# K in place: the score matmuls read 32 consecutive keys at a time, one exp per pair, p turned by four matmuls

## The chip, the cores and the metric

The kernel runs on one core of a Trainium2 chip. The metric is the device time of one execution in microseconds; a kernel is run several times and the median is given. One further execution is profiled. Engines are named as in the profile: PE is TensorE (PEld its weight loads), DVE is VectorE, ACT is ScalarE, POOL is GpSimd, SP is SyncE, which issues the DMAs.

## The reference

Two decode layers, run twice over the same weights and caches. Four tokens (one per batch entry, B = 4), width 448, 16 query heads over 8 key/value heads of size 256, the last 2048 keys of an 8192-key cache, and an FFN of 1792:

```python
W = min(4096, max(256, Sk // 4))                     # 2048
q = (x @ wq).reshape(B, Sq, 16, 256).transpose(0, 2, 1, 3)
k = repeat(k_cache[:, :, Sk - W:, :], 2, axis=1)
v = repeat(v_cache[:, :, Sk - W:, :], 2, axis=1)
p = softmax(einsum("bhqd,bhkd->bhqk", q, k) * 256 ** -0.5)
o = einsum("bhqk,bhkd->bhqd", p, v)
attention = o.transpose(0, 2, 1, 3).reshape(B, Sq, 4096) @ wo
ffn = (silu(x @ w_gate) * (x @ w_up)) @ w_down

x = x + attention(layernorm(x)); x = x + ffn(layernorm(x))
x = x + attention(layernorm(x)); x = x + ffn(layernorm(x))
```

All inputs and the output are bfloat16.

## The kernel before

The unit of work is a *pair*: one token and one key/value head (two query heads) in one of the two layers, so 2 x 4 x 8 = 64 pairs. A token's K and V for one head are 1 MB each and come as two loads of 512 KB each, into `half` buffers (27 of them, 4 KB per partition, shared by K and V). For 5 of 8 heads, K and V loaded in layer 0 are held until the token's pair of layer 1 has used them; the other 3 are loaded again. So 44 pairs load and 20 reuse, and up to 20 of the 27 buffers are held.

A step of the loop is one head: at the ends one pair, in the middle two, the earlier token in layer 1 and the next token in layer 0. When a token has done all 8 heads, its residual, norm, FFN, next norm and query projection (`ffn`, `qproj`, L482 and L523 and L551) come between the pairs.

One pair (`pair`, from L608) goes as follows.

- SP issues two K loads (L616) and two V loads (L629), each waiting for the release of the buffer that it fills. SP's instructions run in order.
- K arrives with 16 consecutive keys per partition, 8 in each half. DVE transposes each half in place in 32 x 32 blocks of 4-byte words (L621), so that partitions run over the head dimension and columns hold the keys. In a half, a column index splits into `(l g c r v)`: `l` (2) and `g` (4) name the key in its partition, `c` the block of the head dimension, `r` (32) the partition that the key came in, `v` the element of the 4-byte word.
- POOL builds `qe` (L646), the query masked so that 8 columns hold the four partition quadrants for two heads. PE computes the scores (L642, `scores`): 32 matmuls, 8 (`ce`) x 2 halves (`hf`) x 2 (`x`). Each has 8 stationary columns and 128 moving columns; the four of one `ce` write to partitions 0, 32, 64 and 96 of one PSUM tile, and the 8 accumulate. This group of 32 is called a burst below.
- DVE takes the maximum over 128 columns (L653), PE spreads it over partitions (L656), DVE makes the bias (L660, L664), ACT takes the exp (L668), once for each half of K, 40 partitions each, into `praw`. In `praw` the columns are ordered `(g r h l)`, so that the two halves alternate in pairs of columns; what a half does not own stays zero.
- PE turns p with two matmuls (L677), `praw` stationary and a selection matrix `selt` moving; ACT copies the result to `pT` (L684). PE sums p (L687), DVE and POOL make the reciprocal (L692, L710).
- PE multiplies by V (L700, `pv`): 16 matmuls of 4 stationary and 256 moving columns, again four side by side in four partition quadrants. ACT and DVE take the sum out (L712, L714), PE flips it (L720), DVE scales it into `oT` (L725), and PE does the output projection of the step (L745).

No order is written out by hand. Each operation is recorded in a graph with an engine, a planned duration, a rank (`pos` and leads such as `SLEAD`) and what it reads and writes. `Graph.schedule` plays this graph with the planned durations, takes on each engine the ready operation of lowest rank, chooses the buffer that is planned to come free first for each load, and so fixes every engine's order and the semaphore waits. Planned durations therefore decide the order on PE and SP. Before, a score burst is planned at `32 * MM` with `MM = 0.034`, an exp at 0.33 and the turn at 0.08 us.

Of the kernel before, what the change touches and what calls it, by code (L numbers as in the profile page):

```python
# [5 lines left out]
ACT = mybir.ActivationFunctionType  # L6
ALU = mybir.AluOpType
AX = mybir.AxisListType
BF16 = mybir.dt.bfloat16
# [24 lines left out]
SLEAD = 2.5  # L34
# [4 lines left out]
NS = 2  # L39
# [8 lines left out]
PE, DVE, SCA, POOL, SP = "pe", "dve", "act", "pool", "sp"  # L48
# [230 lines left out]
def build(nc, A_x, A_k_cache, A_v_cache, A_wq, A_wo, B_x, B_w_gate, B_w_up, B_w_down, out):  # L279
    s0 = A_k_cache.shape[2] - WIN  # L280
    g = Graph()

    with ExitStack() as es:
        def sb(name, shape, dt):
            return es.enter_context(nc.sbuf_tensor(name, shape, dt))
# [5 lines left out]
        wd_sb = sb("wd_sb", [128, NFC, D], BF16)  # L291
        half = [sb(f"half{s}", [128, 8 * DH], BF16) for s in range(NPOOL)]
        identb = sb("identb", [128, 128], BF16)
        onesb = sb("onesb", [128, 1], BF16)
        rab = sb("rab", [128, 129], BF16)
        ra = [rab[:, 1:129], rab[:, 0:128]]
        esel = sb("esel", [128, 4, 4, 32], BF16)
        selt = sb("selt", [128, 2, 4, 2, 2], BF16)
        small = sb("small", [128, 11 + 6 * NS + 4 * NY], FP32)
        nmask = small[:, 9 + 2 * NS + 4 * NY:11 + 2 * NS + 4 * NY]  # L300
        nbias = small[:, 11 + 2 * NS + 4 * NY:11 + 6 * NS + 4 * NY]
# [2 lines left out]
        negm = [small[:, 6 + 2 * i:8 + 2 * i] for i in range(NS)]  # L304
        rs = [small[:, 6 + 2 * (NS + i):8 + 2 * (NS + i)] for i in range(NY)]
        ri = [small[:, 6 + 2 * (NS + NY + i):8 + 2 * (NS + NY + i)] for i in range(NY)]
        qmask = sb("qmask", [128, 4], BF16)
        qc = [sb(f"qc{t}", [128, HKV, 8, 2], BF16) for t in range(B)]
        qe = [sb(f"qe{i}", [128, 8, 4, 2], BF16) for i in range(NQ)]
        qS = sb("qS", [128, 8, 16], BF16)  # L310
# [7 lines left out]
        xb = sb("xb", [128, 4, B], BF16)  # L318
        th = sb("th", [128, 2 * NFC], FP32)
        hT = sb("hT", [128, 2 * NFC], BF16)  # L320
        pmax = [sb(f"pmax{s}", [128, 1], BF16) for s in range(NS)]
        praw = [sb(f"praw{s}", [128, 256], BF16) for s in range(NS)]
        pT = [sb(f"pT{s}", [128, 2, 2, 4, 2, 2], BF16) for s in range(NY)]
        oh = [sb(f"oh{s}", [128, DH], BF16) for s in range(NY)]
        osel = sb("osel", [128, 2], BF16)
        oT = [sb(f"oT{s}", [128, 2, 2, 2], BF16) for s in range(2)]

        def ps(name):
            return es.enter_context(nc.psum_tensor(name, [128, 512], FP32))

        Sb = [ps(f"S{i}") for i in range(NS)]
        Yb = [ps(f"Y{i}") for i in range(NY)]
# [4 lines left out]
        R0 = -100.0  # L337
        MM = MMV
# [24 lines left out]
        for a in range(4):  # L363
            g.op(DVE, 0.1, R0, lambda e, a=a: e.memset(qmask[32 * a:32 * a + 32, a:a + 1], DH ** -0.5), r=("qmask",),
                 w=(f"qmask{a}",))
        ivt = identb[:, :].rearrange("p (h x z n) -> p h x z n", h=2, x=2, n=2)
        for y in range(2):
            for x in range(2):
                g.op(DVE, 0.1, R0, lambda e, y=y, x=x: e.tensor_reduce(
                    selt[:, x, :, y, :], ivt[:, :, x, 0:4, :].rearrange("p h a n -> p a n h"), AX.X, ALU.max),  # L370
                    r=("identb",), w=(f"selt{y}{x}",))
        idq = identb[:, :].rearrange("p (q z n) -> p q z n", q=4, n=2)
        g.op(DVE, 0.2, R0, lambda e: e.tensor_reduce(
            nmask[:, :], idq[:, :, 0:4, :].rearrange("p q a n -> p n q a"), AX.XY, ALU.add), r=("identb",), w=("nmask",))
        for s_ in range(NS):
            g.op(DVE, 0.2, R0, lambda e, s_=s_: e.memset(Sb[s_][:, :], 0.0), w=(f"s{s_}",), bank=(f"S{s_}",))
            g.op(DVE, 0.2, R0, lambda e, s_=s_: e.memset(praw[s_][:, :], 0.0), w=(f"praw{s_}_0", f"praw{s_}_1"))
        for a in range(4):
            g.op(DVE, 0.2, R0, lambda e, a=a: e.tensor_copy(
                esel[:, :, a, :], identb[:, :].rearrange("p (c s) -> p c s", c=4)), r=("identb",), w=(f"esel{a}",))  # L380
# [3 lines left out]
            w=("osel",))  # L384
        g.op(DVE, 0.2, R0, lambda e: e.tensor_reduce(lomask[:, :], iv[:, :, 1, :], AX.XY, ALU.add), r=("identb",),
             w=("lomask",))
# [199 lines left out]
        def x_in(e):  # L586
            last = None
            for cc in range(4):
# [6 lines left out]
             r=("z",), w=tuple(f"x{t}" for t in range(B)), bank=("Z",))  # L595
# [10 lines left out]
        pos = -1  # L606

        def pair(pos, si, side, nside, t, layer, kvh):  # L608
            p_, s_, q_ = pos % NY, pos % NS, pos % NQ
            if layer == 1 and (t, kvh) in k_held:  # L610
                kc, kk = k_held.pop((t, kvh))
            else:
                kc, kk = [[], []], [f"k{pos}_{hf}" for hf in range(2)]
# [21 lines left out]
            def scores(e):  # L635
                last = None
                for ce in range(8):
                    for hf in range(2):
                        kt = half[kc[hf][0]][:, :].rearrange("p (l g c r v) -> p c v g r l", l=2, g=4, c=4, v=2)
                        for x in range(2):  # L640
                            qd = 64 * hf + 32 * x
                            last = e.matmul(Sb[s_][qd:qd + 8, 0:128], lhsT=qe[q_][:, ce, :, :].rearrange("p a n -> p (a n)"),  # L642
                                            rhs=kt[:, ce // 2, ce % 2, 2 * x:2 * x + 2, :, :], start=(ce == 0),
                                            stop=(ce == 7), skip_group_check=True)
                return last
            g.op(POOL, 0.25, pos - SLEAD - 1, lambda e: e.tensor_tensor(  # L646
                qe[q_][:, :, :, :], qc[t][:, kvh, :, :].unsqueeze(2).broadcast_to([128, 8, 4, 2]),
                qmask[:, :].unsqueeze(1).unsqueeze(3).broadcast_to([128, 8, 4, 2]), op=ALU.mult),
                r=(f"qc{t}_{kvh}",) + tuple(f"qmask{a}" for a in range(4)), w=(f"qe{q_}",))
            o = g.op(PE, 32 * MM, pos - SLEAD, scores, r=tuple(kk) + (f"qe{q_}",), w=(f"s{s_}",), bank=(f"S{s_}",))  # L650
            if not keep_k:
                o.rel = tuple(kc)
            g.op(DVE, 0.21, pos, lambda e: e.tensor_reduce(  # L653
                pmax[s_][0:104, :], Sb[s_][0:104, 0:128], AX.X, ALU.max),
                r=(f"s{s_}",), w=(f"pmax{s_}",), bank=(f"S{s_}",))
            g.op(PE, 0.1, pos, lambda e: e.matmul(  # L656
                Sb[s_][0:104, 128:160].rearrange("p (q x) -> p q x", q=4), lhsT=pmax[s_][0:104, 0:1].broadcast_to([104, 104]),
                rhs=identb[0:104, :].rearrange("p (q x) -> p q x", q=4)[:, :, 0:8], start=True, stop=True,
                skip_group_check=True), r=(f"pmax{s_}", "identb"), w=(f"m{s_}",), bank=(f"S{s_}",))
            g.op(DVE, 0.16, pos, lambda e: e.tensor_reduce(  # L660
                negm[s_][0:104, :], Sb[s_][0:104, 128:160].rearrange("p (k n) -> p n k", n=2), AX.X, ALU.max, negate=True),
                r=(f"m{s_}",), w=(f"negm{s_}",), bank=(f"S{s_}",))
            nb = nbias[:, 4 * s_:4 * s_ + 4]
            g.op(DVE, 0.2, pos, lambda e: e.scalar_tensor_tensor(  # L664
                out=nb[0:104, 2:4], in0=negm[s_][0:104, :], scalar=1.0, in1=nmask[0:104, :], op0=ALU.mult, op1=ALU.mult,
                accum_out=nb[0:104, 0:1]), r=(f"negm{s_}", "nmask"), w=(f"nb{s_}",))
            for hf in range(2):
                g.op(SCA, 0.33, pos, lambda e, hf=hf: e.activation(  # L668
                    praw[s_][64 * hf:64 * hf + 40, :].rearrange("p (g r h l) -> p h g r l", g=2, h=2, l=2)[:, hf, :, :, :],
                    Sb[s_][64 * hf:64 * hf + 40, 0:128].rearrange("p (g r l) -> p g r l", g=2, l=2), ACT.Exp,  # L670
                    bias=nb[64 * hf:64 * hf + 40, 0:1]),
                    r=(f"s{s_}", f"nb{s_}"), w=(f"praw{s_}_{hf}",), bank=(f"S{s_}",))

            def turn(e):
                last = None
                for c in range(2):
                    last = e.matmul(Yb[p_][:, 64 + 32 * c:96 + 32 * c], lhsT=praw[s_][0:104, 128 * c:128 * c + 128],  # L677
                                    rhs=selt[0:104, :, :, :, :].rearrange("p x a y n -> p (x a y n)"), start=(c == 0),
                                    stop=False, skip_group_check=True)
                return last  # L680
            g.op(PE, 0.08, pos, turn,
                 r=(f"praw{s_}_0", f"praw{s_}_1") + tuple(f"selt{y}{x}" for y in range(2) for x in range(2)), w=(f"yp{p_}",),
                 bank=(f"Y{p_}",))
            g.op(SCA, 0.2, pos, lambda e: e.activation(  # L684
                pT[p_][:, :, :, :, :, :].rearrange("p c x a y n -> p (c x a y n)"), Yb[p_][:, 64:128], ACT.Copy),
                r=(f"yp{p_}",), w=(f"pT{p_}",), bank=(f"Y{p_}",))
            g.op(PE, 0.05, pos, lambda e: e.matmul(  # L687
                Yb[p_][:, 32:64].rearrange("p (k n) -> p k n", n=2), lhsT=onesb[:, 0:1].broadcast_to([128, 128]),
                rhs=pT[p_][:, :, :, :, :, :].rearrange("p c x a y n -> p y (c x a) n")[:, 0, :, :], start=False,
                stop=False, skip_group_check=True),  # L690
                 r=(f"pT{p_}", "onesb"), w=(f"ysum{p_}",), bank=(f"Y{p_}",))
            g.op(DVE, 0.18, pos, lambda e: e.tensor_reduce(  # L692
                rs[p_][:, :], Yb[p_][:, 32:64].rearrange("p (k n) -> p n k", n=2), AX.X, ALU.add),
                r=(f"ysum{p_}",), w=(f"rs{p_}",), bank=(f"Y{p_}",))

            def pv(e, hv):
                last = None
                for a in range(2):
                    for gg in range(4):
                        last = e.matmul(Yb[p_][32 * gg:32 * gg + 4, 256:512],  # L700
                                        lhsT=pT[p_][:, gg % 2, gg // 2, 2 * hv + a, :, :].rearrange("p y n -> p (y n)"),
                                        rhs=half[vs[hv][0]][:, 1024 * a + 256 * gg:1024 * a + 256 * gg + 256], start=False, stop=False, skip_group_check=True)
                return last
            for hv in range(2):
                kw = dict(acc=(f"y{p_}",)) if hv else dict(w=(f"y{p_}",))
                o = g.op(PE, 0.385, pos, lambda e, hv=hv: pv(e, hv), r=(f"pT{p_}", f"v{t}_{kvh}_{hv}"),
                         bank=(f"Y{p_}",), **kw)
                if not keep_v:
# [4 lines left out]
                 w=(f"oh{p_}",), bank=(f"Y{p_}",))  # L713
# [4 lines left out]
            def flip(e):  # L718
# [9 lines left out]
                r=(f"yo{p_}", f"ri{p_}"), w=(f"oT{si % 2}_{side}",), bank=(f"Y{p_}",))  # L728
# [24 lines left out]
        for si, pairs in enumerate(steps()):  # L753
# [8 lines left out]
            for t, layer in full:  # L762
                pos_ = pos
                pos = pos_ - CROSS
# [12 lines left out]
                pos = pos_  # L777
# [34 lines left out]
def bass_interleave_layers__sliding_block_cached__swiglu_ffn__decode_kernel(  # L812
    nc, A_x, A_k_cache, A_v_cache, A_wq, A_wo, B_x, B_w_gate, B_w_up, B_w_down, out
):
    build(nc, A_x, A_k_cache, A_v_cache, A_wq, A_wo, B_x, B_w_gate, B_w_up, B_w_down, out)
# [28 lines left out]
```

## Time and profile before

| | |
|---|---|
| median of 8 runs | 327.36 us (324.97 to 328.58) |
| profiled execution, its own time | 328.58 us |
| its span, first to last instruction | 326.7 us |
| mean granted TensorE clock | 0.741 of full |
| read from HBM | 104.44 MB, 320 GB/s over the span |
| busy: PE, PEld, DVE, ACT, POOL | 238.4, 169.2, 198.9, 90.9, 85.2 us |
| scores, L642 on PE | 2048 matmuls, 306 ns each |
| K transposes, L621 on DVE | 88, 1239 ns each |
| exp, L668 on ACT | 128, 362 ns each |
| turn, L677 on PE | 128 matmuls, 183 ns each, 101 ns for the weight load |

The span can be cut into 40 slices of 8.17 us; a digit is the busy share of a slice in tenths. "PEclk" is the clock that the throttle granted TensorE in that slice. A matmul's own duration includes its way through the array, and matmuls overlap, so what a row of matmuls costs is read from the time between starts. In a group's line, "x32" is the number of instructions and the number before it the time from the first start to the last end. In the chain of waits, "issue" is time in which an engine waited for nothing that the profile shows, and SPq is SP's queue of DMA issues.

### The profile page before, as it was taken

To read this page: it belongs to the slowest core of one execution; us is meant where nothing else is said; L and a number is where in the kernel's file an instruction comes from. 1 tells how busy PE (TensorE), PEld (TensorE's weight loads), DVE (VectorE), ACT (ScalarE), POOL (GpSimd) and SP (SyncE) were. 2 spreads that over 40 slices of the span, in tenths; PEclk is the share of its full clock that TensorE was granted. 3 is DMA by queue.
4 is the path that set the end of the run, shared out by engine and by line. 5 is a ranking of instruction groups with operands and counts; after the bars stand their busy time and mean duration, and the time that the engine had idled before them with its cause. 6 is when DMAs were issued, how large, how long until landed. Compare 5 with 4: busy or idle time off the path is not lost.

```text
span 326.7 us, 13161 instructions
## 1 busy us (share of the span) xinstructions
PE 238.4 (73%) x5792; PEld 169.2 (52%) x5792; DVE 198.9 (61%) x744; ACT 90.9 (28%) x289; POOL 85.2 (26%) x199
## 2 busy tenths in 40 slices
PE   2656555456578787797588887789878878689965
PEld 1534333244365555485455554566745556576545
DVE  6387556643145889773348798756567983834422
ACT  0313122111013344223143434122333443124510
POOL 2313211112020333223034332304143324134311
PEclk9998556777557999855579999555577997558955
DMA  7999999999989999997689998999599999735000
GB/s 281 391 404 392 393 397 394 393 398 393 395 309 315 378 374 369 402 358 264 243 294 403 400 401 304 398 391 387 195 392 368 350 376 396 256 106 221 2 2 2
DMA packets 42329, 105.28 MB, mean 322 GB/s; under 512 B 3097, under 2 KB 7201, under 8 KB 41889
## 3 DMA queue, kind: packets, MB, share of 16 engines
q1 hardware_dynamic: 42272, 104.45, 85.3%
q8 instruction: 45, 0.74, 0.9%
q14 instruction: 12, 0.09, 0.1%
HBM read 104.44 MB, written 0.00 MB: 320 GB/s over the span
## 4 chain that ended last, share of the span: by engine, by line
PE 34%; DMA 30%; DVE 13%; SPq 12%; issue 6%; ACT 3%
DMA half<-in_A_k_cache_dram 18%; DMA half<-in_A_v_cache_dram 13%; PE S L642 12%; DVE half L621 7%; PE Y L700 7%; SPq L616 6%; PE Z L482 4%; PE A L745 4%; SPq L629 3%; SPq L398 3%; DVE oh L714 2%; ACT praw L668 2%; PE Z L523 2%; PE Y L720 1%; PE Z L431 1%
## 5 line engine op out<-in xcount | busy, mean ns | idle before, releaser
L621 DVE STREAM_TRANSPOSE half<-half 128x1024 uint32<-128x1024 uint32 x88 | 109.1, 1239 | 24.0 <-DMA half<-in_A_k_cache_dram 23.5
L642 PE MATMUL S<-half,qe 128*8 128x128 bf16 x2048 | 84.9, 306 | 13.1 <-ACT praw L668 5.2
L700 PE MATMUL Y<-half,pT 128*4 128x256 bf16 x1024 | 53.3, 323 | 21.4 <-DMA half<-in_A_v_cache_dram 11.8
L642 PEld LDWEIGHTS S<-half,qe 128*8 128x8 bf16 x2048 | 51.8, 89 | 31.3 <-ACT praw L668 8.5
L710 POOL TENSOR_TENSOR small<-small 128x2 f32<-128x2 f32 x64 | 44.3, 696 | 75.9 <-DVE small L692 69.3
L668 ACT ACTIVATE praw<-S,small 40x128 bf16<-40x128 f32 x128 | 46.4, 362 | 46.7 <-DVE small L664 45.2
L712 ACT ACTIVATE oh<-Y 128x256 bf16<-128x256 f32 x64 | 24.4, 381 | 86.2 <-PE Y L700 85.8
L646 POOL TENSOR_TENSOR qe<-qc,qmask 128x64 bf16<-128x64 bf16 x64 | 18.6, 292 | 103.7 <-PE S L642 87.6
L653 DVE TENSOR_REDUCE pmax<-S 104x1 bf16<-104x128 f32 x64 | 18.4, 287 | 39.5 <-PE S L642 39.3
L714 DVE SCALAR_TENSOR_TENSOR oh<-oh,small,Y 128x256 bf16<-128x256 bf16 x64 | 30.0, 472 | 15.0 <-ACT oh L712 14.7
L700 PEld LDWEIGHTS Y<-half,pT 128*4 128x4 bf16 x1024 | 21.1, 86 | 29.3 <-DMA half<-in_A_v_cache_dram 13.4
L745 PE MATMUL A<-oT,wo_sb 128*128 128x1 bf16 (+1 forms) x688 | 24.3, 165 | 5.0 <-DVE oT L725 4.0
L745 PEld LDWEIGHTS A<-oT,wo_sb 128*128 128x128 bf16 x688 | 21.0, 99 | 11.2 <-DVE oT L725 6.1
L684 ACT ACTIVATE pT<-Y 128x64 bf16<-128x64 f32 x64 | 13.9, 222 | 45.5 <-PE Y L677 36.7
L720 PE MATMUL Y<-osel,oh 128*128 128x2 bf16 x128 | 12.2, 170 | 12.3 <-DVE oh L714 12.3
L687 PE MATMUL Y<-pT,onesb 128*128 128x32 bf16 x64 | 12.1, 191 | 9.6 <-ACT pT L684 9.5
L720 PEld LDWEIGHTS Y<-osel,oh 128*128 128x128 bf16 x128 | 7.6, 103 | 20.8 <-DVE oh L714 16.2
L449 POOL TENSOR_SCALAR st<-st 128x1 f32<-128x1 f32 x16 | 4.2, 265 | 50.5 <-DVE st L437 39.0
L482 PE MATMUL Z<-xn,wq_sb 128*128 128x1 bf16 (+1 forms) x480 | 15.5, 166 | 1.0 <-DMA wq_sb<-in_A_wq_dram 0.7
L656 PE MATMUL S<-identb,pmax 104*104 104x32 bf16 x64 | 13.4, 229 | 2.6 <-DVE pmax L653 1.1
L687 PEld LDWEIGHTS Y<-pT,onesb 128*128 128x128 bf16 x64 | 6.8, 108 | 15.9 <-ACT pT L684 12.4
L482 PEld LDWEIGHTS Z<-xn,wq_sb 128*128 128x128 bf16 x480 | 14.2, 104 | 1.5 <-DMA wq_sb<-in_A_wq_dram 0.8
(81 smaller groups left out, 232.6 us busy)
## 6 DMA issues: line engine op xcount, KB each, us to landing
half<-in_A_k_cache_dram SPq DMA_DIRECT2D x88, 512.0 KB, 7.3
half<-in_A_v_cache_dram SPq DMA_DIRECT2D x88, 512.0 KB, 7.2
wo_sb<-in_A_wo_dram SPq DMA_DIRECT2D x8, 448.0 KB, 12.4
wq_sb<-in_A_wq_dram SPq DMA_DIRECT2D x3, 1024.0 KB, 7.0
wd_sb<-in_B_w_down_dram SPq DMA_DIRECT2D x1, 1568.0 KB, 16.2
wg_sb<-in_B_w_gate_dram SPq DMA_DIRECT2D x1, 1344.0 KB, 14.2
wu_sb<-in_B_w_up_dram SPq DMA_DIRECT2D x1, 1344.0 KB, 14.7
wq_sb<-in_A_wq_dram SPq DMA_DIRECT2D x1, 512.0 KB, 10.4
```

The source lines that it names most:

```text
L482: last = e.matmul(o, lhsT=lhsT, rhs=rhs, start=(cc == 0 and hh == 0 and ee == 0), stop=(cc == 3), skip_group_check=True)
L616: g.dma(pos - KLEAD, 1 << 19, lambda e, cell=cell, hf=hf: e.dma_start(half[cell[0]][:, :], ksrc[:, 2048 * hf:2048 * hf + 2048]), None, w=( ...
L621: return e.transpose(a, a)
L642: last = e.matmul(Sb[s_][qd:qd + 8, 0:128], lhsT=qe[q_][:, ce, :, :].rearrange("p a n -> p (a n)"), rhs=kt[:, ce // 2, ce % 2, 2 * x:2 * x ...
L668: g.op(SCA, 0.33, pos, lambda e, hf=hf: e.activation(praw[s_][64 * hf:64 * hf + 40, :].rearrange("p (g r h l) -> p h g r l", g=2, h=2, l=2 ...
L687: g.op(PE, 0.05, pos, lambda e: e.matmul(Yb[p_][:, 32:64].rearrange("p (k n) -> p k n", n=2), lhsT=onesb[:, 0:1].broadcast_to([128, 128]), ...
L700: last = e.matmul(Yb[p_][32 * gg:32 * gg + 4, 256:512], lhsT=pT[p_][:, gg % 2, gg // 2, 2 * hv + a, :, :].rearrange("p y n -> p (y n)"), r ...
L710: g.op(POOL, 0.25, pos, lambda e: e.tensor_tensor(ri[p_][:, :], rs[p_][:, :], expo[:, 1:3], op=ALU.pow), r=(f"rs{p_}", "expo"), w=(f"ri{p_ ...
L712: g.op(SCA, 0.28, pos, lambda e: e.activation(oh[p_][:, :], Yb[p_][:, 256:512], ACT.Copy), r=(f"y{p_}",), w=(f"oh{p_}",), bank=(f"Y{p_}",))
L714: g.op(DVE, 0.4, pos, lambda e: e.scalar_tensor_tensor(out=oh[p_][:, :], in0=oh[p_][:, :], scalar=lomask[:, 0:1], in1=Yb[p_][:, 256:512], ...
L720: last = e.matmul(Yb[p_][:, 2 * dh:2 * dh + 2], lhsT=oh[p_][:, :].rearrange("p (m e) -> p e m", e=2)[:, dh, :], rhs=osel[:, :], start=Fals ...
L745: last = e.matmul(Av[:, cc, sl], lhsT=wo_sb[:, 4 * kvh + k, c0:c0 + 128], rhs=oT[si % 2][:, k % 2, k // 2, 0:n], start=False, stop=False, ...
```

## The change

The score matmuls read their moving operand in the order `(g l r)` instead of `(g r l)`: innermost, 32 keys that lie two elements apart, where before two keys 1024 elements apart alternated. The scores therefore stand in PSUM in another order, and the exp puts them back: it reads PSUM as `(g l r)` permuted to `g r l`, 32 words apart innermost. One exp now does both halves of K on partitions 0 to 103. Since both halves then lie in the same columns of `praw` (two columns wider, the first two zero), the turn has a selection matrix for each half and reads `praw` once from column 2 on and once from column 0 on, which moves the second half by two columns: four matmuls instead of two. The planned durations become 0.8, 0.38 and 0.12 us. Some one-column tiles share one tile, `tiny`.

```diff
-        onesb = sb("onesb", [128, 1], BF16)
+        tiny = sb("tiny", [128, 8 + NS], BF16)
+        onesb, qmask, osel = tiny[:, 0:1], tiny[:, 2:6], tiny[:, 6:8]
+        pmax = [tiny[:, 8 + s:9 + s] for s in range(NS)]
...
-        selt = sb("selt", [128, 2, 4, 2, 2], BF16)
+        selt = [sb(f"selt{h}", [128, 2, 4, 2, 2], BF16) for h in range(2)]
...
-        praw = [sb(f"praw{s}", [128, 256], BF16) for s in range(NS)]
+        praw = [sb(f"praw{s}", [128, 258], BF16) for s in range(NS)]
...
-        for y in range(2):
-            for x in range(2):
-                g.op(DVE, 0.1, R0, lambda e, y=y, x=x: e.tensor_reduce(
-                    selt[:, x, :, y, :], ivt[:, :, x, 0:4, :].rearrange("p h a n -> p a n h"), AX.X, ALU.max),
-                    r=("identb",), w=(f"selt{y}{x}",))
+        for h in range(2):
+            for y in range(2):
+                for x in range(2):
+                    g.op(DVE, 0.1, R0, lambda e, h=h, y=y, x=x: e.tensor_copy(selt[h][:, x, :, y, :], ivt[:, h, x, 0:4, :]),
+                         r=("identb",), w=(f"selt{h}{y}{x}",))
...
-                        kt = half[kc[hf][0]][:, :].rearrange("p (l g c r v) -> p c v g r l", l=2, g=4, c=4, v=2)
+                        kt = half[kc[hf][0]][:, :].rearrange("p (l g c r v) -> p c v g l r", l=2, g=4, c=4, v=2)
...
-            o = g.op(PE, 32 * MM, pos - SLEAD, scores, r=tuple(kk) + (f"qe{q_}",), w=(f"s{s_}",), bank=(f"S{s_}",))
+            o = g.op(PE, 0.8, pos - SLEAD, scores, r=tuple(kk) + (f"qe{q_}",), w=(f"s{s_}",), bank=(f"S{s_}",))
...
-            for hf in range(2):
-                g.op(SCA, 0.33, pos, lambda e, hf=hf: e.activation(
-                    praw[s_][64 * hf:64 * hf + 40, :].rearrange("p (g r h l) -> p h g r l", g=2, h=2, l=2)[:, hf, :, :, :],
-                    Sb[s_][64 * hf:64 * hf + 40, 0:128].rearrange("p (g r l) -> p g r l", g=2, l=2), ACT.Exp,
-                    bias=nb[64 * hf:64 * hf + 40, 0:1]),
-                    r=(f"s{s_}", f"nb{s_}"), w=(f"praw{s_}_{hf}",), bank=(f"S{s_}",))
+            g.op(SCA, 0.38, pos, lambda e: e.activation(
+                praw[s_][0:104, 2:258].rearrange("p (g r h l) -> p h g r l", g=2, h=2, l=2)[:, 0, :, :, :],
+                Sb[s_][0:104, 0:128].rearrange("p (g l r) -> p g r l", g=2, l=2), ACT.Exp, bias=nb[0:104, 0:1]),
+                r=(f"s{s_}", f"nb{s_}"), w=(f"praw{s_}",), bank=(f"S{s_}",))
 
             def turn(e):
                 last = None
                 for c in range(2):
-                    last = e.matmul(Yb[p_][:, 64 + 32 * c:96 + 32 * c], lhsT=praw[s_][0:104, 128 * c:128 * c + 128],
-                                    rhs=selt[0:104, :, :, :, :].rearrange("p x a y n -> p (x a y n)"), start=(c == 0),
-                                    stop=False, skip_group_check=True)
+                    for h in range(2):
+                        c0 = 128 * c + 2 - 2 * h
+                        last = e.matmul(Yb[p_][:, 64 + 32 * c:96 + 32 * c], lhsT=praw[s_][0:104, c0:c0 + 128],
+                                        rhs=selt[h][0:104, :, :, :, :].rearrange("p x a y n -> p (x a y n)"),
+                                        start=(c == 0 and h == 0), stop=False, skip_group_check=True)
                 return last
-            g.op(PE, 0.08, pos, turn,
+            g.op(PE, 0.12, pos, turn,
...
```

## The prediction

> **What bounds the kernel now.** I read the 40 slices first, then the chain of waits, then busy time by stage, then the order of instructions around single bursts. "DMA" and "GB/s" in the slices say when the loads run at their full rate, "PEclk" which clock TensorE was granted.
>
> ```profile
> PEclk9998556777557999855579999555577997558955
> DMA  7999999999989999997689998999599999735000
> GB/s 281 391 404 392 393 397 394 393 398 393 395 309 315 378 374 369 402 358 264 243 294 403 400 401 304 398 391 387 195 392 368 350 376 396 256 106 221 2 2 2
> PE 34%; DMA 30%; DVE 13%; SPq 12%; issue 6%; ACT 3%
> DMA half<-in_A_k_cache_dram 18%; DMA half<-in_A_v_cache_dram 13%; PE S L642 12%; DVE half L621 7%; PE Y L700 7%; SPq L616 6%; PE Z L482 4%; PE A L745 4%; SPq L629 3%; SPq L398 3%; DVE oh L714 2%; ACT praw L668 2%; PE Z L523 2%; PE Y L720 1%; PE Z L431 1%
> ```
>
> A full slice moves about 398 GB/s. At that rate the 104.44 MB take 262 us; the last load lands near 302 us. So some 35 us are lost while loads wait for a free buffer, and 25 us more follow the last load. No change on the engines can win more than about 35 us plus what it takes off that tail. By stage (busy us and instructions of PE, PEld, DVE, ACT, POOL, then clock, DMA share, GB/s):
>
> ```profile
> 88.00:112.00 24.00, 19.23 (x483) 13.92 (x483) 13.29 (x43) 6.22 (x20) 5.23 (x13) 0.70 0.92 333
> 139.00:172.00 33.00, 26.11 (x660) 19.14 (x660) 16.22 (x63) 9.04 (x29) 7.94 (x19) 0.57 0.81 291
> 172.00:194.00 22.00, 18.32 (x446) 12.40 (x446) 18.92 (x68) 8.37 (x28) 8.75 (x20) 1.00 1.04 402
> 278.00:302.00 24.00, 20.27 (x531) 15.78 (x535) 13.58 (x66) 6.20 (x20) 6.95 (x19) 0.60 0.54 193
> ```
>
> Where DMA falls behind (88 to 112, 139 to 172, 212 to 242, 278 to 302), DVE has much idle time and PE has most of the work: projections and FFN of a finished token stand between the pairs, and a pair that reuses held K and V costs PE as much as one that loads. From 172 to 194 loads run at 402 GB/s, and a faster PE is worth nothing.
>
> The chain, read piece by piece, has 26 score bursts (L642) in the stages that stay below 380 GB/s (88 to 112, 139 to 172, 194 to 302 us) and two after 302 us. I count these 28; those before 88 and from 112 to 139 us I leave out, since loads are as fast as they get there. By the clock granted when each starts, 9 of the 28 run at full clock, 19 at half.
>
> **Scores.** The first two lines are from the timeline of PE near 107 us (clock 1.00), the next two near 164 us (0.50), the last near 168 us (1.00):
>
> ```profile
> 107.01 1.04 PE L700 MATMUL Y<-half,pT 128*4 128x256 bf16 x32
> 108.49 1.31 PE L642 MATMUL S<-half,qe 128*8 128x128 bf16 x32 [0.44 <-ACT praw L668]
> ...
> 164.09 1.88 PE L700 MATMUL Y<-half,pT 128*4 128x256 bf16 x32
> 165.98 1.32 PE L642 MATMUL S<-half,qe 128*8 128x128 bf16 x32
> ...
> 168.76 0.32 PEld L745 LDWEIGHTS A<-oT,wo_sb 128*128 128x128 bf16 x10 [0.29 <-issue]
> ```
>
> Both kinds are eight groups of four matmuls in four column tiles that run side by side. Less the last matmul's own time and by seven steps, a group of PV (256 columns in a row) takes (1.04 - 0.27)/7 = 0.110 us at full and (1.88 - 0.42)/7 = 0.208 us at half clock: it follows the clock. A score group has half the columns, yet takes (1.31 - 0.31)/7 = 0.143 us at both clocks. So something other than the array sets it, and what differs is the read: innermost, it jumps 1024 elements and back with each key. The new order steps two elements, 32 times. PV's rate would make 128 columns 0.104 us at half clock, 0.055 at full. How fast a moving read of step two runs, no row shows; bounds are 0.143 (nothing gained) and PV's rate. L482 loads weights with step two, L745 without, and both start every 27 ns at half clock, so a step of two need not cost: I take PV's rate at half clock. At full clock the issue may limit: L745 starts one weight load per (0.32 - 0.10)/9 = 0.025 us, four are 0.100. No row has pairs of load and matmul faster than this, so I take 0.100, and 0.055 as the end. A burst saves 7 x 0.039 = 0.27 us at half, 7 x 0.043 = 0.30 at full clock (0.62 at the end): 19 x 0.27 + 9 x 0.30 = 7.8 us, at best 10.7.
>
> The Trainium skill (TensorE: Matmul & The Clock Gate, "Wait — 56ns, not 53.3ns?") states a floor of about 25 ns from start to start, however small the matmul. It speaks against the gain at full clock. The trace has the four matmuls of a PV group starting within 10 ns, but no four groups faster than 27 ns a matmul on average. By the rule the scores are worth the 7.8 us, without it 10.7.
>
> **Exp.** Two instructions of 362 ns become one of the same 128 elements on 104 partitions. Its PSUM read now steps 32 words inside. L490 reads 16 elements four words apart in 274 ns and 12 adjacent ones in 270, so a stepped read at 0 to twice the price per element; L684 and L712 (222 ns for 64, 381 for 256) make an element 0.83 ns, so at worst 128 x 0.83 = 0.11 us more, and I take none. From 88 us the chain holds 16 exps; half of them go: 8 x 0.36 = 2.9 us (2.0 at worst). Other exps hide behind PE, and ACT is busy 28%: nothing is won there.
>
> ```profile
> L668 ACT ACTIVATE praw<-S,small 40x128 bf16<-40x128 f32 x128 | 46.4, 362 | 46.7 <-DVE small L664 45.2
> ```
>
> **Turn.** Two more matmuls a pair, each with a 128-column weight load at 25 to 27 ns: 0.054 us on PE, before pT can be copied. On 28 chain pairs 1.5 us lost (0 if they fall into PE's waits, 64 x 0.054 = 3.5 at most).
>
> **Order and start.** Planner costs alter: scores move ahead of flips and out-projections in places, SP issues some K loads before V loads from its 70th line on. Each SP instruction waits for its buffer with all later loads behind it. After 60 us the chain has almost no SPq, so I take 0 and +/-3 us as bounds, a DMA-late load (L700 waits 11.8 us in all for V) being the nearest row. Four more setup copies on DVE (0.16 us each) lie under the wq load: nothing; uncovered, 0.6 us.
>
> **Program fetch.** This takes some back. The queue lines have 45 instruction packets (first line below), and PE has 2 x 5792 instructions, loads and matmuls: 257 to a packet. Counted in the trace, PE's longest stops without a releaser stand before its instructions 2498, 4546, 5058, 8130 and 9666, all multiples of 256 apart. PE has run ahead of its program there. The worst, as the chain has it:
>
> ```profile
> q8 instruction: 45, 0.74, 0.9%
> ...
> 158.26 1.06 PE S L642 x23
> 159.32 3.60 issue
> 162.92 0.48 PE S L642 x3
> ```
>
> From 88 us on, nine such stops (0.4 to 3.9 us) sum to 13.9 us. The blocks of 256 that end in the five longest took 5.9 to 9.3 us, yet one that met no stop took 3.7: the packet comes at no fixed time. A faster PE reaches the boundary sooner and waits for the same packet. A block holds 4096/11584 of 256 in score instructions, 64 to a burst, so 1.4 bursts; nine blocks return 9 x 1.4 x (0.27 - 0.054) = 2.7 us. The turn adds 4 x 64 = 256 instructions, one more packet. Bounds: 0 to 9 us; I take 2.7.
>
> **Sum.** -7.8 - 2.9 + 1.5 + 2.7 = -6.5, and shorter pairs free K and V buffers earlier in just the stages that starve, which is the same time, not more. The profiled execution took 328.58 us (span 326.7), 1.2 above the median of 327.36, so the change is put on the median: 320.9, say 321.
>
> **Rivals.**
> 1. *The read runs at PV's rate at both clocks, and nothing is lost at boundaries*: -10.7 - 2.9 + 1.5 = -12.1, 315; with the turn hidden (1.5) and a quarter of the stops gone (3.5), 310. For: groups of PV start within 10 ns. Against: the 25 ns row.
> 2. *The step of two elements is as slow as the jump*: the burst keeps 0.143 a group. -2.9 + 1.5 leaves -1.4, 326. For: no row has a stepped moving read. Against: L482's loads.
> 3. *Program fetch becomes the bound (slower)*: savings wait at the boundaries, the one extra block comes on top. It decides from 6.5 + 2.7 = 9.2 us of returned time on, when stops grow from 13.9 to over 23 us, for instance four more of the 159 us kind (2.3 to 3.6 us). With six of them, 6 x 2.5 = 15 us, it ends at 327.4 - 9.2 + 15 = 333. For: boundaries already hit. Against: most blocks in the dense stretches pass without a stop.
>
> The granted clock adds spread. Shorter bursts may look idler: PV at half clock costs a pair 4 x 0.098 = 0.39 us more, 3.5 us if all nine full-clock chain pairs lost it. The Trainium skill (same page, "What's actually happening") has the gate set by how busy PE was in the last 3.4 us; by it, a lost full clock is the likelier direction. The trace's PEclk swings while PE is about equally busy, so I give it no term.
>
> **Numbers.** Forecast 0.50; rival 1 0.22; rival 2 0.12; rival 3 0.16. A measurement of this kernel tells apart about 0.5%, 1.6 us. Faster: 0.50 + 0.22 + 0.03 of rival 2 = 0.75. Same 0.10 (rival 2 and a mild rival 3), slower 0.15. The range takes in rival 1 to its 310 and reaches up past rival 2 into rival 3: 310 to 330.
>
> **What would show it.** Right: score bursts of 32 spanning near 1.05 us at both clocks, or about 0.7 at full clock (rival 1); one exp per pair near 362 ns; turns 0.05 us longer; slices near 139 to 172 and 278 to 302 with more GB/s. Wrong: bursts still 1.3 us (rival 2); score bursts shorter while "issue" in the chain grows past 6% (rival 3); an exp over 470 ns; a mean clock well under 0.74.

## The result, and the profile after

The changed kernel takes 324.05 us (median of 22 runs, 321.66 to 328.92) where the kernel before takes 327.6 us (59 runs): a ratio of 0.9895, 95% interval [0.9874, 0.9916], so 3.4 us faster, with 6.5 forecast. A ratio leaves out the runs that took over 1.5% longer than the fastest of the same kernel. Run once more, beside the last experiments, the changed kernel gave 0.9926 [0.9892, 0.9960]. The profiled execution took 322.47 us, span 320.6; the profiled one of before took 328.58, so the two profiles stand further apart than the medians.

The slices of the page, clock and load rate, and the chain:

```profile
PEclk9999999999999875555556757555587755557765
GB/s 271 403 407 393 392 397 396 391 394 397 390 367 175 387 401 392 364 386 390 389 163 331 402 401 398 384 333 370 334 383 401 400 387 399 224 81 252 4 2 2
PE 38%; DMA 30%; SPq 13%; DVE 9%; issue 7%; ACT 2%; POOL 1%; ACTq 0%
DMA half<-in_A_k_cache_dram 17%; DMA half<-in_A_v_cache_dram 13%; PE Y L699 10%; PE S L641 10%; SPq L615 6%; PE Z L481 4%; DVE half L620 4%; PE A L744 3%; SPq L628 3%; SPq L397 3%; PE Z L522 3%; DVE oh L713 2%; PE Z L550 2%; PE Y L719 1%; PE Y L676 1%
```

The line numbers are one lower than before from the score loop on, two lower at the exp, one at PV. Read three things. Scores fall from 40 to 31 us in the chain (12% and 10%), as meant. PV (the multiplication by V) rises from 22 to 32 us (7% and 10%), although nothing in PV was changed. And the long stretches at full clock of before (slices 13 to 17 and 21 to 25) are gone. A second profile of the changed kernel, of an execution of 326.91 us, has 34 us of PV but also 39 us of scores in its chain: the rise of PV comes back, the fall of scores does not, since another path can end last. What the scores gained is read from single bursts below. The first 9s of PEclk mean nothing: the throttle's first record stands at 102 us, and PV at 88 us takes 0.62 us for eight matmuls, which is half clock. So the mean granted clock of 0.729 against 0.741 hides most of the change; PV's duration shows it.

The groups, busy us and mean ns of one, PV of before first:

```profile
L700 PE MATMUL Y<-half,pT 128*4 128x256 bf16 x1024 | 53.3, 323 | 21.4 <-DMA half<-in_A_v_cache_dram 11.8
...
L699 PE MATMUL Y<-half,pT 128*4 128x256 bf16 x1024 | 63.9, 375 | 17.0 <-DMA half<-in_A_v_cache_dram 14.8
L641 PE MATMUL S<-half,qe 128*8 128x128 bf16 x2048 | 63.7, 290 | 13.1 <-issue 9.7
L666 ACT ACTIVATE praw<-S,small 104x128 bf16<-104x128 f32 x64 | 22.6, 366 | 47.5 <-DVE small L663 47.5
L676 PE MATMUL Y<-selt,praw 104*128 104x32 bf16 x256 | 17.0, 187 | 0.0
```

A PV matmul shows about 271 ns at full and 415 ns at half clock, so the mean tells the mixture: 323 ns before, 375 now. Counted, 620 of 1024 ran at full clock before and 224 now. By stage (same columns as in the prediction; the first line is the kernel before, which the prediction does not show for this stage):

```profile
112.00:139.00 27.00, 20.53 (x502) 13.23 (x498) 23.07 (x77) 10.32 (x32) 7.82 (x16) 0.96 1.02 382
...
112.00:139.00 27.00, 23.00 (x556) 15.37 (x560) 23.01 (x78) 7.80 (x25) 8.93 (x18) 0.56 1.03 389
139.00:172.00 33.00, 27.71 (x713) 21.14 (x709) 19.35 (x78) 6.38 (x22) 8.66 (x23) 0.50 0.89 318
278.00:296.00 18.00, 15.53 (x444) 12.58 (x445) 8.06 (x50) 4.46 (x16) 7.21 (x19) 0.57 0.54 176
```

From 139 to 172 us the loads move 318 instead of 291 GB/s, as forecast, while PE is busier (27.7 against 26.1 us), not idler: it does more in the stage, at half clock. From 278 us on there is no such rise (176 against 193 GB/s). From 112 to 139 us the clock went from 0.96 to 0.56.

Bursts and PV in the timeline of PE, near 104 us at full and near 127 us at half clock:

```profile
103.48 0.63 PE L641 MATMUL S<-half,qe 128*8 128x128 bf16 x32
105.33 1.05 PE L699 MATMUL Y<-half,pT 128*4 128x256 bf16 x32
...
126.52 1.02 PE L699 MATMUL Y<-half,pT 128*4 128x256 bf16 x16 [0.28 <-DVE small L691]
127.62 1.02 PE L641 MATMUL S<-half,qe 128*8 128x128 bf16 x32
```

From first to last start a burst takes 0.72 us at half clock (median of 45) and 0.42 at full (median of 7), against 1.01 at either before. Seven steps make a group of four 0.102 and 0.060 us, close to what PV's rate makes of half the columns (0.104 and 0.055). The read now follows the clock.

### The profile page after: what moved, and what is told of

It reads as the page before. It is cut to its first block, busy times and chain, and to the rows that moved or that the text cites. A ratio compares the mean times of both kernels' runs of the same rounds, so it can differ in the third digit from the quotient of the medians.

```text
span 320.6 us, 13355 instructions
## 1 busy us (share of the span) xinstructions
PE 234.0 (73%) x5920; PEld 170.6 (53%) x5920; DVE 199.1 (62%) x748; ACT 66.5 (21%) x225; POOL 85.3 (27%) x199
## 4 chain that ended last, share of the span: by engine, by line
PE 38%; DMA 30%; SPq 13%; DVE 9%; issue 7%; ACT 2%; POOL 1%; ACTq 0%
DMA half<-in_A_k_cache_dram 17%; DMA half<-in_A_v_cache_dram 13%; PE Y L699 10%; PE S L641 10%; SPq L615 6%; PE Z L481 4%; DVE half L620 4%; PE A L744 3%; SPq L628 3%; SPq L397 3%; PE Z L522 3%; DVE oh L713 2%; PE Z L550 2%; PE Y L719 1%; PE Y L676 1%
## 5 line engine op out<-in xcount | busy, mean ns | idle before, releaser
L699 PE MATMUL Y<-half,pT 128*4 128x256 bf16 x1024 | 63.9, 375 | 17.0 <-DMA half<-in_A_v_cache_dram 14.8
L641 PE MATMUL S<-half,qe 128*8 128x128 bf16 x2048 | 63.7, 290 | 13.1 <-issue 9.7
L641 PEld LDWEIGHTS S<-half,qe 128*8 128x8 bf16 x2048 | 46.5, 111 | 20.4 <-issue 11.7
L645 POOL TENSOR_TENSOR qe<-qc,tiny 128x64 bf16<-128x64 bf16 x64 | 18.6, 293 | 88.7 <-PE S L641 74.7
L652 DVE TENSOR_REDUCE tiny<-S 104x1 bf16<-104x128 f32 x64 | 18.3, 288 | 33.4 <-PE S L641 33.2
L666 ACT ACTIVATE praw<-S,small 104x128 bf16<-104x128 f32 x64 | 22.6, 366 | 47.5 <-DVE small L663 47.5
L683 ACT ACTIVATE pT<-Y 128x64 bf16<-128x64 f32 x64 | 13.9, 222 | 49.5 <-PE Y L676 45.6
L719 PE MATMUL Y<-tiny,oh 128*128 128x2 bf16 x128 | 13.0, 172 | 13.8 <-DVE oh L713 13.3
L719 PEld LDWEIGHTS Y<-tiny,oh 128*128 128x128 bf16 x128 | 8.0, 106 | 23.4 <-DVE oh L713 18.3
L686 PE MATMUL Y<-pT,tiny 128*128 128x32 bf16 x64 | 12.5, 200 | 7.8 <-ACT pT L683 7.7
L481 PE MATMUL Z<-xn,wq_sb 128*128 128x1 bf16 (+1 forms) x480 | 15.6, 166 | 2.7 <-DVE st L436 2.2
L676 PE MATMUL Y<-selt,praw 104*128 104x32 bf16 x256 | 17.0, 187 | 0.0
L655 PE MATMUL S<-identb,tiny 104*104 104x32 bf16 x64 | 14.8, 245 | 2.6 <-DVE tiny L652 2.2
```

The costliest lines, as they stand in the source:

```text
L481: last = e.matmul(o, lhsT=lhsT, rhs=rhs, start=(cc == 0 and hh == 0 and ee == 0), stop=(cc == 3), skip_group_check=True)
L666: g.op(SCA, 0.38, pos, lambda e: e.activation(praw[s_][0:104, 2:258].rearrange("p (g r h l) -> p h g r l", g=2, h=2, l=2)[:, 0, :, :, :], ...
L699: last = e.matmul(Yb[p_][32 * gg:32 * gg + 4, 256:512], lhsT=pT[p_][:, gg % 2, gg // 2, 2 * hv + a, :, :].rearrange("p y n -> p (y n)"), r ...
L719: last = e.matmul(Yb[p_][:, 2 * dh:2 * dh + 2], lhsT=oh[p_][:, :].rearrange("p (m e) -> p e m", e=2)[:, dh, :], rhs=osel[:, :], start=Fals ...
```

## The experiments

All ratios are to the kernel before, run on the same chip. "Stops" are PE's waits without a releaser at multiples of 256 instructions, counted in the trace from 60 us on, from start to start, where they are over 0.38 us: 12.8 us before, 15.6 in the changed kernel (17.0 in its second profile). (The 13.9 of the prediction includes one of 1.1 us that also carries a semaphore.)

### The read alone, in the old order

```diff
-  kt = half[...].rearrange("p (l g c r v) -> p c v g r l", ...)
+  kt = half[...].rearrange("p (l g c r v) -> p c v g l r", ...)
-  Sb[s_][64 * hf:64 * hf + 40, 0:128].rearrange("p (g r l) -> p g r l", g=2, l=2), ACT.Exp,
+  Sb[s_][64 * hf:64 * hf + 40, 0:128].rearrange("p (g l r) -> p g r l", g=2, l=2), ACT.Exp,
```

> The kernel before with the new read order alone: scores read (g l r), the two exps stay and read PSUM permuted, two turn matmuls, planned durations and so the order of every engine as before. Theory clock (the faster read leaves PE's array idle more of the time, so the clock gate grants half clock for longer, and PV pays back part of the gain): score bursts near 1.03 us at half and 0.64 at full clock, fewer full-clock stretches than before, PV mean from 323 to 360 to 380 ns, time 1 to 3 us under before. Theory fetch (the saved time is returned at program packets): PV mean stays near 323 ns, the stops at packet boundaries sum to well over 14 us. Theory order (what the changed planned durations did to the order costs most of the gain): here the order is the old one, so the full gain of the scores, 6 to 8 us.

Measured: 0.9936 [0.9900, 0.9972], 2.1 us. Bursts as in the changed kernel, exps 363 ns, PV's mean 388 ns (136 of 1024 at full clock), stops 13.3 us. PV's group:

```profile
L700 PE MATMUL Y<-half,pT 128*4 128x256 bf16 x1024 | 65.9, 388 | 23.5 <-DMA half<-in_A_v_cache_dram 12.0
```

The read alone takes the full clock away: theory clock, with even more of it lost than expected (360 to 380 ns). Theory order, which asked for 6 to 8 us here, is out.

### The old read with one exp and four turns

```diff
-  kt = half[...].rearrange("p (l g c r v) -> p c v g l r", ...)
+  kt = half[...].rearrange("p (l g c r v) -> p c v g r l", ...)
-  o = g.op(PE, 0.8, pos - SLEAD, scores, ...)
+  o = g.op(PE, 32 * MM, pos - SLEAD, scores, ...)
-  Sb[s_][0:104, 0:128].rearrange("p (g l r) -> p g r l", g=2, l=2), ACT.Exp, ...
+  Sb[s_][0:104, 0:128].rearrange("p (g r l) -> p g r l", g=2, l=2), ACT.Exp, ...
```

> The changed kernel with the old read order (g r l) and nothing else: one exp, four turn matmuls, its own planned durations and so its own order on PE and SP. Bursts 1.3 us at both clocks in every theory. Theory clock: the slow read keeps the array occupied, so the full-clock stretches come back (112 to 136 and 167 to 205 us or thereabouts) and PV's mean falls to 325 to 340 ns; time 1 to 2 us under before (exp 2.9 less turn 1.5), so 325.5 to 326.5. Theory fetch: stops at packet boundaries near 14 us or fewer, since PE is as slow as before; time also 326. Theory order: 328 or more, since the new order's cost stands without the scores' gain.

The expectation says that it has the changed kernel's order. It has not: the scores' planned duration was put back as well, and the order on PE is neither kernel's. Measured: 1.0035 [1.0000, 1.0071]; PV's mean 323 ns, 620 matmuls at full clock, stops 9.8 us.

```profile
L699 PE MATMUL Y<-half,pT 128*4 128x256 bf16 x1024 | 52.6, 323 | 21.3 <-DMA half<-in_A_v_cache_dram 15.4
```

The full clock comes back with the slow read. The time says less than was meant, but it is no sign of a gain from the exp and the turn.

### The order alone

```diff
-  o = g.op(PE, 32 * MM, pos - SLEAD, scores, ...)
+  o = g.op(PE, 0.8, pos - SLEAD, scores, ...)
-  g.op(SCA, 0.33, pos, lambda e, hf=hf: e.activation(
+  g.op(SCA, 0.19, pos, lambda e, hf=hf: e.activation(
-  g.op(PE, 0.08, pos, turn,
+  g.op(PE, 0.12, pos, turn,
```

(The four setup reductions are planned at 0.2, as long as eight copies.)

> The kernel before, its instructions unchanged, put into the changed kernel's order by its planned durations (scores 0.8, exps 0.19 each, turn 0.12): SP's order is the same as in the changed kernel, PE's but for 49 instructions. Theories clock and fetch: order is neutral, 327 to 328 us. Theory order: 329 to 332, or, if the order is what won, 324.

Measured: 1.0019 [0.9982, 1.0056], PV's mean 326 ns. With the old read the order is neutral.

### Extra array time to hold the clock

```diff
+  def fill(e):
+      for _ in range(2):
+          last = e.matmul(Sb[s_][:, 160:512], lhsT=identb[:, :], rhs=wq_sb[:, 0:352], start=False, stop=False, ...)
+      return last
+  g.op(PE, 0.3, pos, fill, r=("identb", "wq0", f"praw{s_}"), w=(f"s{s_}",), bank=(f"S{s_}",))
```

> The changed kernel with two extra matmuls a pair after the turn, 352 columns each over the whole array, into columns of the score bank that nobody reads: they add nothing to the output, 0.6 us a pair of array time at half clock, 0.3 at full. Theory clock: the array is busier, full clock is granted in the dense stretches, PV's mean falls under 330 ns, more than half of the bursts after 100 us run in 0.64 us; PE gains 0.39 (PV) and 0.3 (scores) a pair and pays 0.3; time 319 to 323. Theory fetch: the clock may rise but 256 more instructions bring one more packet and the stops stay or grow: 324 or more. If neither, the extra matmuls at half clock cost 28 x 0.6 x about a half: 330.

Measured: 1.0157 [1.0084, 1.0231]. PV's group:

```profile
L705 PE MATMUL Y<-half,pT 128*4 128x256 bf16 x1024 | 56.9, 344 | 17.2 <-DMA half<-in_A_v_cache_dram 13.3
```

The clock can be bought: 468 PV matmuls at full clock instead of 224. But not to the extent expected (under 330 ns), and the price is higher than the gain. The price is not array time alone: the extra matmuls are 256 more instructions, and being planned they move PE's order too. The same with one extra matmul (`range(1)`, planned 0.15):

> e4_fill with one extra matmul of 352 columns a pair in place of two, which adds nothing to the output. Theory clock, with the extra array time paid in full: between the changed kernel and e4_fill in both, full clock 50 to 80 us, PV mean 350 to 370 ns, time 327 to 331. If one is enough to tip the gate, full clock near 85 us at half the price: 324 to 326.

Measured: 0.9983 [0.9943, 1.0023], 372 PV matmuls at full clock, PV 355 ns. Between the two, as expected without a tipping point.

### Exp and turn, in one order

The order kernel with the new read, in the same two lines as in the first experiment:

> The kernel e5_order with the new read order: old instructions otherwise (two exps of 40 partitions, two turn matmuls), the changed kernel's order. With e5_order (slow read, old exp and turn), e2_exp_turn (slow read, new exp and turn) and the changed kernel (fast read, new exp and turn) it makes a square in one order. If exp and turn are worth the 1.4 us of the prediction once the read is fast, it stands 1.4 us over the changed kernel, at 325.4; if they are worth nothing, as the slow side says (e2_exp_turn 1.0035, e5_order 1.0019 of before), it equals it, 324. Theory clock: full clock under 60 us, PV mean 370 to 390 ns.

Measured: 0.9824 [0.9749, 0.9899], a wide interval from three runs (the median of all six, 324.26 us, would make it 0.987); PV's mean 383 ns, stops 7.2 us. Since its interval touches the changed kernel's, both were run again on one chip:

> The changed kernel once more, beside e13_read_order on one chip. 0.9895 of before by its earlier runs; the same again, 0.987 to 0.992.

> e6_read_order once more (new read order, two exps, two turn matmuls, the changed kernel's order). If merging the exps for two more matmuls is worth its 1.4 us, it stands 1.4 us over e11_changed; if it is worth nothing, level within 1 us; if the 256 instructions of the turn, one packet, cost more than the exp wins, 1 to 3 us under e11_changed and the best version here (0.982 by three earlier runs).

Measured: 0.9926 [0.9892, 0.9960] and 0.9869 [0.9830, 0.9907]. PV in the second:

```profile
L700 PE MATMUL Y<-half,pT 128*4 128x256 bf16 x1024 | 69.1, 396 | 18.3 <-DMA half<-in_A_v_cache_dram 14.4
```

Side by side, as ratios to the kernel before ("order" is PE's, ACT's and DVE's; the changed kernel's order on PE differs from the new one here in 49 instructions):

| instructions | old order | new order |
|---|---|---|
| old read, two exps, two turns | 1 | 1.0019 |
| new read, two exps, two turns | 0.9936 | 0.9869 (0.9824) |
| new read, one exp, four turns | not run | 0.9926, 0.9895 |

The read is worth 2.1 us in the old order and 4.9 to 6.4 us in the new one. With the new read the order is no longer neutral: the same instructions take 2.2 us less in the new order, or 0.5 to 3.9 us if the two intervals are combined. One exp and four turns in place of two and two are worth nothing or less: 1.9 us slower where both were run on one chip, with intervals that overlap a little. The version with two exps and two turns is the fastest measured that computes everything, 323.6 us, though its lead over the changed kernel is not settled. The second expectation counted e2 as a corner of the square; for the reason given it is not one.

### The plan fitted to half clock

```diff
-  o = g.op(PE, 0.385, pos, lambda e, hv=hv: pv(e, hv), ...)
+  o = g.op(PE, 0.52, pos, lambda e, hv=hv: pv(e, hv), ...)
```

> The changed kernel with PV planned at 0.52 in place of 0.385 us for eight matmuls, which is nearer to what half clock makes of it; only the order moves. Theory clock: the plan now fits the clock that is granted, scores and PV fall in other places; 0 to 2 us faster than the changed kernel, PV's mean unchanged at 365 to 390. Theory order (the placement is a matter of chance): anything between 321 and 329 us.

Measured: 0.9982 [0.9947, 1.0016], 2.8 us slower than the changed kernel; 20.4 us of stops, PV's mean 385 ns. A plan nearer to the truth made a slower order: theory order, and a loss, where theory clock had hoped for a gain.

### What PE time is still worth

```diff
-  for ce in range(8):
+  for ce in range(4):
```

> The changed kernel with the last four of the eight groups of each score burst left out (half of the head dimension is missing from the scores), in the same order: 512 fewer loads and matmuls on half of the columns, a burst of 0.29 us from first to last start at half clock in place of 0.72. It asks what PE time is still worth. Theory clock: the array is even idler, full clock falls under 25 us, PV mean 395 to 415 ns; PE saves 0.43 a pair and pays 0.1 to 0.2, so 4 to 7 us under the changed kernel. Theory fetch: 2048 fewer instructions are eight packets fewer, stops fall under 8 us, time 10 us under. If PE is no longer what binds: within 2 us of the changed kernel.

Measured: 0.9435 [0.9376, 0.9493], 310.3 us, some 15 us under the changed kernel. PV's mean is 402 ns, half clock nearly throughout (the page's 0.961 is again the missing record). Theory clock's 4 to 7 us fell: more than array time had been removed. Stops are down to 2.2 us. (The 512 of the expectation is a slip: 1024 weight loads and 1024 matmuls are left out, the 2048 instructions that it names after.) Two runs separate array time and program length:

```diff
-  last = e.matmul(Sb[s_][qd:qd + 8, 0:128], ..., rhs=kt[:, ce // 2, ce % 2, 2 * x:2 * x + 2, :, :], ...)
+  last = e.matmul(Sb[s_][qd:qd + 8, 0:64], ..., rhs=kt[:, ce // 2, ce % 2, 2 * x, :, :], ...)
```

> The changed kernel with 64 moving columns in place of 128 in every score matmul (the scores of half of the keys are missing): the array time of e9_half, all instructions of the changed kernel, same order. Theory array (PE's array time is what e9_half won): stands with e9_half, 309 to 313 us, although the program is as long as before. Theory fetch (e9_half won by its eight missing packets): 2 to 5 us under the changed kernel, 319 to 322, stops at packet boundaries still over 10 us.

```diff
-  last = e.matmul(Sb[s_][qd:qd + 8, 0:128], ..., rhs=kt[:, ce // 2, ce % 2, 2 * x:2 * x + 2, :, :], ...)
+  for gi in range(2):
+      last = e.matmul(Sb[s_][qd:qd + 8, 64 * gi:64 * gi + 64], ..., rhs=kt[:, ce // 2, ce % 2, 2 * x + gi, :, :], ...)
```

> The changed kernel with every score matmul split into two of 64 columns: same array time, 4096 more instructions on PE, so 16 more packets; nothing is left out, same order. Theory array: within 2 us of the changed kernel, 322 to 326. Theory fetch: stops over 25 us, 333 to 345. If the issue of load and matmul binds (no sustained rate under 15 ns a pair was seen), a burst lasts longer than 0.72 us at half clock, and part of a slower time is that.

Measured: 0.9763 [0.9731, 0.9796] (320.0 us) with half the columns and the whole program; 1.1287 [1.1232, 1.1343] (369.0 us, well beyond the 345 expected at most) with all columns and 4096 more instructions. Packets and the score group, first of half the columns, then of the split:

```profile
q8 instruction: 46, 0.75, 1.0%
L641 PE MATMUL S<-half,qe 128*8 128x64 bf16 x2048 | 40.9, 237 | 16.2 <-issue 12.7
```

```profile
q8 instruction: 62, 1.02, 1.1%
PE 44%; issue 16%; DMA 15%; SPq 13%; DVE 9%; ACT 2%; POOL 1%; DVEq 0%; ACTq 0%
L642 PE MATMUL S<-half,qe 128*8 128x64 bf16 x4096 | 70.0, 236 | 38.1 <-issue 33.0
```

And a piece of the split kernel's chain:

```profile
127.48 0.85 PE S L642 x53
128.33 2.50 issue
130.82 0.39 PE S L642 x11
```

A burst of 64 split matmuls takes 0.79 us from first to last start when nothing stops it, against 0.72 of 32 whole ones: nearly the same, at most 64 x 0.08 = 5 us in all. What is new are 28 stops of 52.9 us in all, every one of them at a multiple of 256 instructions from the next; issue makes 16% of the chain. The 16 packets cost 45 us less those 5, so 2.5 to 2.8 us each, or 2.2 if the clock that PV lost too (48 matmuls at full clock in place of 224, 4.3 us of PE time) is taken off.

The traces also hold the packets themselves, 16 KB each, in q8. From 60 us on, in the kernel before, the changed and the split kernel alike, each stop ends 1.2 to 1.6 us after the landing of a packet, and a packet starts only after PE has passed the boundary before it: 2.7 to 2.9 us after it on average while loads run (up to 6.9), 0.2 to 1.1 us once the last load has landed. That PE waits for its program at these places is read from this, not only argued from the count.

On the other side, e9_half and e10_cols64 have much the same array time in a burst (0.29 and 0.36 us at half clock) and eight packets between them: 0.9763 - 0.9435 is 10.7 us, 1.3 us a packet, or 0.8 if 64 x 0.07 us of array time are taken off. Halving the array time alone was worth 4.3 us (0.9895 to 0.9763), with 204 more PV matmuls at half clock (5 us of PE time) and stops risen to 22.9 us: the faster PE loses clock and waits for its program.

## Why the prediction was right and where it was wrong

The time moved as forecast, by about half of the 6.5 us. That 324 us lies between 310 and 330 says little, since the time before lies there too; what counts is how the terms fared, and their errors partly cancelled, which was luck.

**Scores, half clock: right.** 0.72 us from first to last start against 0.104 x 7 = 0.73. **Full clock: too careful.** The end of 0.055 us a group is the true one (0.060), not the 0.100 from the rate of L745. The scores do not share that row's limit; L745 loads 128 columns each time and a score matmul 8, but that this is the reason was not shown. The Trainium skill's floor of 25 ns from start to start (TensorE: Matmul & The Clock Gate, "Wait — 56ns, not 53.3ns?") does not hold for four column tiles side by side: 0.060/4 is 15 ns, and the 64-column bursts come to 358/7/4 = 13 ns at half and 222/7/4 = 8 ns at full clock (three bursts). It mattered little, as full clock became rare.

**Why the old read was slow** stands as argued: the order of the read was the only difference to the scores in the first experiment, and the time per group went from 0.144 us at both clocks to the array's rate. The Trainium skill (SBUF — State Buffer, "Door 1: The DMA port swizzle (why [64,N] ≈ [32,N])") has SBUF lines of 16 bytes and wants two hits in a line; the old order left the line at every key, the new one reads four keys in it. The runs agree, but no step in between was tried, so the size of a line is not shown here.

**The clock: the step that got no term.** The prediction priced a lost full clock at 0.39 us a pair and 3.5 us in all, and gave it nothing since PEclk seemed to follow no busy share. It follows the read. 396 of 1024 PV matmuls lost full clock, 25 pairs by 16, 25 x 0.39 = 9.7 us of PE time; the chain's PV grew by 10 us. (In the second profile 116 are left at full clock, so 504 lost it.) Every kernel with the slow read (before, e2_exp_turn, e5_order) has PV at 323 to 326 ns, every one with the fast read and no extra matmuls at 375 to 402. In windows of 3.41 us the difference shows at the same work: a window at half clock with one pair (32 score and 16 PV matmuls) was followed by full clock at 51, 58, 65 and 72 us in the kernel before, and at 44, 51, 58 and 65 us in the changed one by half (where no clock is recorded yet, but L686 takes 209 ns there, against 190 for the same matmul, L687, in the windows at full clock before). What the gate counts exactly was not settled.

**Read in all: about right in the new order, too much in the old.** 7.8 less 2.7 for the program was forecast, 5.1; measured are 4.9 to 6.4 us in the new order and 2.1 in the old. Too little for full clock, nothing for the lost clock: two errors of opposite sign.

**Exp and turn: the term that was mis-sized.** -2.9 + 1.5 was forecast, -1.4; measured is +1.9 us on one chip, 0.2 to 3.6 with both intervals. The exp itself is as forecast (363 ns with the stepped PSUM read against 362, and 366 on 104 partitions), and it is 24 us less of ACT work. The exps all but left the chain (5.7 us before, 0.7 after), more than was counted, and still no time was won: what leaves the chain need not leave the time. The turn's 256 instructions are one more packet, which by the two runs above costs 0.8 to 2.8 us, and the two profiles with two turns have 7.2 and 8.3 us of stops where the changed kernel's two have 15.6 and 17.0. That this packet is the reason was argued from these numbers, not shown by itself.

**Order: right with the old read only** (neutral, 1.0019); with the new read the new order won 2.2 us, and e7_plan's lost 2.8, so the bounds of 3 us were fair. One reading behind it was wrong: SP issues its 195 DMAs in the same order in both kernels, by their lines in the two traces. PE, ACT and DVE change their order. (A slip that nothing rests on: 302 less 262 leaves 40 us of waiting for buffers, less some 2 before the first load, not 35.)

**Program fetch: right.** Stops rose by 2.8 us (4.2 in the second profile), 2.7 had been taken. The sign named for rival 3, "issue" past 6% of the chain, hardly tells: it was 6.3% before and is 7% after. Rival 3's mechanism decides as soon as the program grows: the chain of the changed kernel already has it inside a burst,

```profile
223.25 0.43 PE S L641 x16
223.68 2.30 issue
225.99 0.60 PE S L641 x16
```

and the split kernel, 16 packets on, is what rival 3 described. Rival 2 (a slow read at step two) is out.

## What to carry to other kernels

A kernel of many small matmuls can be bound by the fetch of its own program: count the engine's instructions, look for stops at one fixed multiple, and prefer a change that removes instructions (here 0.8 to 2.8 us per 256) to one that makes each faster and adds some. When a matmul's time does not follow the granted clock, look at the order of its moving read; when it is mended, look whether the other matmuls have lost full clock, as they did here, and read the clock from a matmul's duration instead of the page's mean. And price a change in the order in which it will run: the same read was worth 2.1 us in one order and 4.9 in another.

## What was unexpected of the hardware

- The faster read cost full clock: with it, 24 to 44 us of recorded full clock in an execution (3 to 17 in e9_half, e10_cols64 and e12_split), with the slow read 130 to 140 us. Buying part of it back with extra matmuls (for two a pair an estimated 0.3 to 0.6 us, by PV's rate) cost more than it brought.
- Column tiles side by side sustain a load and a matmul every 15 ns at 128 columns and every 8 ns at 64 (three bursts), at full clock.
- TensorE's program arrives in packets of 256 instructions, and PE stands for up to 4 us where one is late. The packet starts later while loads run (2.7 to 2.9 us after the boundary on average) than after them (0.2 to 1.1 us, four or five packets in each trace). The split of 2048 matmuls at nearly the same array time made the kernel 13% slower than the one before.
